# Block attention and a gated feed-forward layer on one core: the first attention units, the weight conversion and the first group in one written-out order

## The chip, the cores and the metric

The kernel runs on one core of one Trainium2 chip. Its time is the device time of one execution in microseconds. The core has five engines with a queue each, served in order: TensorE (PE in the profile, its weight loads PEld), VectorE (DVE), ScalarE (ACT), GpSimd (POOL) and SyncE (SP), which here issues all DMAs.

## What is computed

Attention over 4 batches of 8 heads, 768 tokens, head size 64. Each query sees the keys within 16 positions and, beside them, one summary key (the maximum) and one summary value (the mean) for each of 24 blocks of 32 tokens. The result, 3072 tokens by 512, goes through two matrix products with an activation between them.

```
scores_l = where(mask_l, scale * q @ k.T, -1e9)
scores_s = scale * q @ k_sum.T + log(32)        # k_sum: maximum of 32 keys
a = softmax(concat(scores_l, scores_s))
x = a @ concat(v, v_sum)                        # v_sum: mean of 32 values
h = x @ w_in                                    # 512 x 2048
g = h * tanh(log1p(exp(h)))
out = g @ w_out                                 # 2048 x 512
```

The weights come as 64-bit floats. The kernel turns each into two 32-bit parts, a high one and a low one, and does the same with x and g, so every product of the feed-forward layer is three matmuls: high by high, high by low, low by high.

## The kernel before

**Attention.** A chunk is 256 tokens of one batch (three to a batch), a unit is a chunk and a pair of heads: 12 x 4 = 48 units. A unit's work runs through the engines: scores on TensorE (`att_scores`, tile sc); mask, scale and maximum in four VectorE reductions (L279); four exponentials on ScalarE (L284); two small VectorE ops rs and the multiply of the scores by it on GpSimd (`att_normalize`, L293 to L295); a transpose on TensorE with a ScalarE copy to tile pt (`att_transpose`); the product with the values (`att_values`, x_ps), from which ScalarE makes xh and VectorE xl. The first chunk of a batch also needs km, the maximum of its keys, and vq, the mean of its values, both VectorE reductions; for batch 0 the mean is a TensorE product vm_ps. GpSimd copies km into the loaded tile qk (L225).

**Weights.** There are 16 blocks of w_in and 16 of w_out, 512 KB each in 64 bits. `load_weight` does all of a block: the DMA; on VectorE L119 and L120 (tile w_x), on ScalarE L122 (w_f), on VectorE L123 and L125, on ScalarE the copy to the high part (L127) and on GpSimd the subtraction that gives the low part (L128).

**Feed-forward.** A step in the later groups is one weight block for 512 tokens (a group is two chunks, six groups in all): `ff_in` with 12 matmuls into ph, `ff_act` (Mish on ScalarE into a), `ff_split` (ah, then al = a - ah on VectorE), and two steps later `ff_out` with 12 matmuls into four PSUM tiles po. Group 0 is done in 24 half steps of 256 tokens and two weight blocks each: the first chunk begins, the second follows four half steps behind. In group 0 ah is a ScalarE copy, later a VectorE one.

**What sets the order.** The begin and the 24 half steps of group 0 are placed by a scheduler that looks at when data is ready; the letters in the list of `begins` and the loop only give the sequence in which it is told of them. From the first step of group 1 on, the order is the program's (`manual_schedule`). Units of the next group stand at every second step of a group. Tiles come from rings (pools with a tag and a number of buffers); an instruction that writes a ring's next tile waits for the last reader of the tile that lay there.

Of the kernel before, what the change touches and what calls it, by code (L numbers as in the profile page):

```python
# [20 lines left out]
P = 128  # L21
# [15 lines left out]
NP_ = NFC // 2  # L37
LEAD = 4
# [19 lines left out]
def fused_kernel(ctx: ExitStack, tc: tile.TileContext, q0, qk, kt, v0, vw, vs, w_in, w_out, out):  # L58
# [4 lines left out]
    stage = ctx.enter_context(tc.tile_pool(name="stage", bufs=3))  # L63
# [3 lines left out]
    ff = ctx.enter_context(tc.tile_pool(name="ff", bufs=6))  # L67
# [42 lines left out]
    def load_weight(src, hi, lo, name):  # L110
        t = stage.tile([P, WP], I64, tag="stage", name=name)
        nc.sync.dma_start(t, src)
        words = t.bitcast(U32).rearrange("p (f two) -> p f two", two=2)
        low, high = words[:, :, 0], words[:, :, 1]
        f = ff.tile([P, WP], F32, tag="t", name=f"{name}_f")
        x = ff.tile([P, WP], F32, tag="t", name=f"{name}_x").bitcast(U32)
        u = f.bitcast(U32)

        nc.vector.tensor_scalar(out=x, in0=low, scalar1=29, scalar2=None, op0=ALU.logical_shift_right)  # L119
        nc.vector.scalar_tensor_tensor(out=x, in0=high, scalar=SIGN, in1=x,  # L120
                                       op0=ALU.bitwise_and, op1=ALU.bitwise_or)
        nc.scalar.activation(f, high.bitcast(F32), AF.Copy, scale=2.0 ** -OFFSET)  # L122
        nc.vector.tensor_scalar(out=f, in0=f, scalar1=-_as_f32(F32_MAX), scalar2=_as_f32(F32_MAX),  # L123
                                op0=ALU.max, op1=ALU.min)
        nc.vector.scalar_tensor_tensor(out=u, in0=u, scalar=3, in1=x,  # L125
                                       op0=ALU.logical_shift_left, op1=ALU.bitwise_or)
        nc.scalar.copy(hi, f)  # L127
        nc.gpsimd.tensor_sub(lo, f, hi.bitcast(F32))  # L128
# [36 lines left out]

    sources = {}

    def load_summaries(b, hp):

        ks = stage.tile([P, S], F32, tag="stage", name=f"ks{b}_{hp}")  # L170
        nc.sync.dma_start(ks, kt[b, hp])
        vsum = stage.tile([VP, BLK, BLK], F32, tag="stage", name=f"vsum{b}_{hp}")
        nc.sync.dma_start(vsum, vs[b, hp].rearrange("p (d j) -> p d j", j=BLK))
        sources[b, hp] = ks, vsum

    def key_summaries(b, hp):
# [11 lines left out]
        return ks  # L188

    def value_summaries(b, hp):  # L190
        vm = att.tile([KA, P], F32, tag="vm", name=f"vm{b}_{hp}", bufs=HP + 2)[KW:KA]
        summary[b, hp].append(vm)
        if b == 0:

            vwt = first_att.tile([KA, NQ, P], F32, tag="vw", name=f"vw{b}_{hp}")
            nc.sync.dma_start(vwt[0:KW], vw[b, hp].rearrange("p (s k) -> p s k", s=NQ))
            units[0, hp]["v"] = vwt
            t = first_att.tile([P, NR, P], F32, tag="v0", name=f"v{b}_{hp}", bufs=HP)
            nc.sync.dma_start(t, v0[hp].rearrange("p (j d) -> p j d", d=P))
            ps = att_psum(0, f"vm_ps{b}_{hp}")  # L200
            for j in range(NQ + NR):
                nc.tensor.matmul(ps[KW:KA, 0:P], *((blocks[0:KW, j, :], vwt[0:KW, j, :]) if j < NQ else  # L202
                                                   (blocks[:, j, :], t[:, j - NQ, :])),
                                 start=(j == 0), stop=(j == NQ + NR - 1))
# [4 lines left out]
        nc.vector.reduce_sum(vq, vsum, axis=AX.X)
# [87 lines left out]
    def att_transpose(c, hp):  # L297
# [4 lines left out]
        pt = att.tile([KA, NQ, P], F32, tag="pt", name=f"pt{c}_{hp}")  # L302
# [24 lines left out]
    def parts(step):  # L327

        if len(step) == 2:
            return [step[1]], step[0], 0, TG  # L330
        _, c, fp = step
        return [2 * fp, 2 * fp + 1], 0, c * CH, CH

    def ff_in(step):
        fcs, g, at0, n = parts(step)
        xh, xl = (x[:, :, at0:at0 + n] for x in xs[g])
        ph = ps_w.tile([P, len(fcs), n], F32, tag="w", name=f"ph{step[0]}_{step[-1]}_{at0}")
        for j, fc in enumerate(fcs):
            wh, wl = (weight(0, part, fc) for part in range(2))
            for cc in range(NCC):  # L340
                for k, (w, x) in enumerate(((wh, xh), (wh, xl), (wl, xh))):
                    nc.tensor.matmul(ph[:, j, :], w[:, cc * P:(cc + 1) * P], x[:, cc, :],  # L342
                                     start=(cc == 0 and k == 0), stop=(cc == NCC - 1 and k == 2))
        st[step] = ph.rearrange("p j t -> p (j t)")

    def ff_act(step):

        name = f"{step[0]}_{step[1]}_{step[-1]}"
        a = ff.tile([P, TG], F32, tag="t", name=f"a{name}")
        nc.scalar.activation(a, st[step], AF.Mish)  # L350
        st[step] = a, *(ff.tile([P, TG], F32R, tag=f"a{part}", name=f"a{part}{name}", bufs=3) for part in "hl")

    def ff_split(step):

        a, ah, al = st[step]

        (nc.scalar.copy if len(step) == 3 else nc.vector.tensor_copy)(ah, a)  # L357
        nc.vector.tensor_sub(al, a, ah.bitcast(F32))  # L358

    def ff_out(step):  # L360
        _, ah, al = st.pop(step)
        fcs, g, at0, n = parts(step)
        for t in range(n // P):
            row = g * TG + at0 + t * P
            if fcs[0] == 0:
                po[row] = ps_o.tile([P, DM], F32, tag="o", name=f"po{row}")
            for j, fc in enumerate(fcs):
                tok = slice(j * n + t * P, j * n + (t + 1) * P)
                wh, wl = (weight(1, part, fc) for part in range(2))
                for k, (a, w) in enumerate(((ah, wh), (al, wh), (ah, wl))):  # L370
                    nc.tensor.matmul(po[row], a[:, tok], w,  # L371
                                     start=(fc == 0 and k == 0), stop=(fc == NFC - 1 and k == 2))
            if fcs[-1] == NFC - 1:
                o = ff.tile([P, DM], F32, tag="t", name=f"o{row}")
                (nc.vector.tensor_copy if t % 2 else nc.scalar.copy)(o, po.pop(row))
                nc.sync.dma_start(out[row:row + P, :], o)
# [4 lines left out]
    steps = [(0, c, i - c * LEAD) for i in range(NP_ + LEAD) for c in range(CG) if 0 <= i - c * LEAD < NP_]
    first_steps = len(steps)
    steps += [(g, fc) for g in range(1, NG) for fc in range(NFC)]
# [3 lines left out]
    begins = {"K": lambda n: att_load_keys(0, n), "V": lambda n: att_load_values(0, n),  # L387
              "S": lambda n: (att_scores(0, n), att_normalize(0, n)), "T": lambda n: att_transpose(0, n),
              "A": lambda n: att_values(0, n), "W": load_weights, "L": lambda n: att_load(1, n)}
    for what in "K0 K1 S0 W1 K2 V0 S1 W1 T0 K3 V1 S2 A0 T1 W1 V2 S3 A1 T2 V3 A2 T3 W1 L0 A3".split():  # L390
# [109 lines left out]
```

## Time and profile before

| | |
|---|---|
| three runs | 693.78 us (692.79 to 695.2) |
| profiled execution | 693.84 us, of which the span of its instructions 692.1 us |
| busy, share of the span | TensorE 94%, VectorE 44%, ScalarE 50%, GpSimd 16% |
| chain that ended last | TensorE 81%, VectorE 9%, ScalarE 3%, DMA 3% |

A share is a mean over stages. The page cuts the span into 40 slices of 17.3 us; until about the ninth, TensorE has gaps and the other engines are busiest, and from there on TensorE is busy in nearly every tenth. The trace can be asked for the busy time of each engine in any stretch, for the chain of waits, and for the single instructions in order of time. A busy time of TensorE contains the pipelining of its matmuls, so starts are compared with starts.

### The profile page before, as it was taken

Reading aid. Unit: us, or ns where it says so; the run is one execution under the profiler, and the core shown is the slowest. Engines: PE = TensorE matmul, PEld = TensorE weight load, DVE = VectorE, ACT = ScalarE, POOL = GpSimd, SP = SyncE. Lnnn points to the kernel's source line nnn. Section 1 sums busy time; section 2 is a strip of 40 time slices with the busy share of each in tenths; the row PEclk is TensorE's granted clock in tenths of the full one; section 3 lists DMA queues with packets and bytes.
Section 4 is the critical chain, followed back from the end, with each engine's and each line's share of the span. In section 5 each row is a group of like instructions: output and inputs, shape, how many; then the busy total and the mean of one; then the engine's idle time right before and its main releaser. Section 6 shows DMA issues by size and latency. Waiting matters only on the chain.

```text
span 692.1 us, 11422 instructions
## 1 busy us (share of the span) xinstructions
PE 651.8 (94%) x4352; PEld 525.5 (76%) x4352; DVE 301.4 (44%) x884; ACT 347.7 (50%) x764; POOL 113.6 (16%) x151
## 2 busy tenths in 40 slices
PE   4876598979999999999999999999999999999997
PEld 3665476768878878878878788788788788888885
DVE  5689998883333233453232243453242232221121
ACT  3767758888754555465454464464454454111111
POOL 3444453451101001001001001001010010000000
PEclk9998789999999999999999999999999999999999
DMA  9755555764322132452122151423141110010001
GB/s 292 237 183 174 180 186 174 233 183 127 94 78 85 45 103 70 123 171 89 44 71 62 45 188 57 152 70 89 44 150 44 45 58 1 16 45 1 1 0 61
DMA packets 30678, 70.48 MB, mean 102 GB/s; under 512 B 4768, under 2 KB 9504, under 8 KB 30624
## 3 DMA queue, kind: packets, MB, share of 16 engines
q1 hardware_dynamic: 30624, 69.76, 32.1%
q8 instruction: 34, 0.56, 0.3%
q14 instruction: 20, 0.16, 0.1%
HBM read 61.15 MB, written 6.29 MB: 97 GB/s over the span
## 4 chain that ended last, share of the span: by engine, by line
PE 81%; DVE 9%; ACT 3%; DMA 3%; issue 1%; SPq 0%; POOL 0%; DVEq 0%; ACTq 0%
PE po L371 36%; PE ph L342 35%; PE x_ps L319 4%; PE sc L264 3%; PE pt_ps L301 3%; DVE w_x L119 2%; DVE w_x L120 2%; DVE w_f L123 2%; DVE w_f L125 1%; DMA w<-w_out 1%; PE vm_ps L202 1%; DMA vw<-vw 1%; ACT pr L284 1%; ACT L350 1%; DMA vsum<-vs 1%
## 5 line engine op out<-in xcount | busy, mean ns | idle before, releaser
L350 ACT ACTIVATE a<-ph 128x512 f32<-128x512 f32 x96 | 57.5, 598 | 189.3 <-PE ph L342 189.1
L295 POOL TENSOR_TENSOR pr<-pr,rs 128x480 f32<-128x480 f32 x48 | 50.4, 1050 | 391.1 <-DVE rs L294 347.5
L371 PE MATMUL po<-w_early_out_hi,ah 128*128 128x512 f32 x240 | 98.9, 418 | 12.6 <-ACT ah L357 12.4
L342 PE MATMUL ph<-xh,w_early_in_hi 128*128 128x512 f32 (+1 forms) x280 | 103.9, 371 | 1.6 <-ACT xh L320 1.6
L357 DVE CAST ah<-a 128x512 fp32r<-128x512 f32 x80 | 34.0, 425 | 159.4 <-ACT a L350 159.4
L371 PE MATMUL po<-w_early_out_hi,al 128*128 128x512 f32 x240 | 98.4, 410 | 4.9 <-DVE al L358 4.9
L342 PE MATMUL ph<-xl,w_early_in_hi 128*128 128x512 f32 (+1 forms) x280 | 101.3, 362 | 0.4 <-DVE xl L321 0.2
L342 PE MATMUL ph<-xh,w_early_in_lo 128*128 128x512 f32 (+1 forms) x280 | 101.2, 361 | 0.0
L371 PE MATMUL po<-w_early_out_lo,ah 128*128 128x512 f32 x240 | 96.8, 403 | 0.0
L321 DVE TENSOR_TENSOR xl<-x_ps,xh 128x256 fp32r<-128x256 f32 x48 | 20.2, 421 | 158.3 <-ACT xh L320 158.3
L284 ACT ACTIVATE pr<-pr,nm 128x120 f32<-128x120 f32 x192 | 73.6, 384 | 2.9 <-DVE nm L279 2.3
L358 DVE TENSOR_TENSOR al<-a,ah 128x512 fp32r<-128x512 f32 x96 | 66.5, 692 | 12.6 <-ACT ah L357 9.6
L350 ACT ACT_TABLE_LOAD x44 | 56.5, 1283 | 28.5 <-issue 14.8
L371 PEld LDWEIGHTS po<-w_early_out_hi,ah 128*128 128x128 f32 x240 | 46.0, 194 | 27.0 <-ACT ah L357 14.6
L303 ACT COPY pt<-pt_ps 120x512 f32<-120x512 f32 x48 | 28.2, 587 | 70.8 <-PE pt_ps L301 70.8
L342 PE MATMUL ph<-xh,w_late_in_hi 128*128 128x512 f32 (+1 forms) x168 | 61.8, 368 | 0.0
L342 PEld LDWEIGHTS ph<-xh,w_early_in_hi 128*128 128x128 f32 x280 | 53.1, 190 | 10.7 <-ACT xh L320 2.1
L342 PE MATMUL ph<-xh,w_late_in_lo 128*128 128x512 f32 (+1 forms) x168 | 60.6, 361 | 0.0
L342 PE MATMUL ph<-xl,w_late_in_hi 128*128 128x512 f32 (+1 forms) x168 | 60.4, 359 | 0.0
L342 PEld LDWEIGHTS ph<-xl,w_early_in_hi 128*128 128x128 f32 x280 | 53.2, 190 | 9.2 <-DVE xl L321 1.2
L371 PEld LDWEIGHTS po<-w_early_out_hi,al 128*128 128x128 f32 x240 | 47.1, 196 | 16.4 <-DVE al L358 7.4
L342 PEld LDWEIGHTS ph<-xh,w_early_in_lo 128*128 128x128 f32 x280 | 52.8, 189 | 8.9 <-issue 0.2
(76 smaller groups left out, 1055.0 us busy)
## 6 DMA issues: line engine op xcount, KB each, us to landing
qk<-qk SPq DMA_DIRECT2D x44, 496.0 KB
vw<-vw SPq DMA_DIRECT2D x48, 192.0 KB
w<-w_in SPq DMA_DIRECT2D x16, 512.0 KB
w<-w_out SPq DMA_DIRECT2D x16, 512.0 KB
ks<-kt SPq DMA_DIRECT2D x16, 384.0 KB
out<-o SPq DMA_DIRECT2D x24, 256.0 KB
vsum<-vs SPq DMA_DIRECT2D x12, 384.0 KB
vw<-vm SPq DMA_DIRECT2D x44, 48.0 KB
```

The lines of the kernel that those rows point to most:

```text
L264: nc.tensor.matmul(ps[h][row, at0:at0 + KA], u["qk"][r, s, h * QT:(h + 1) * QT], u["qk"][r, s, P:], start=True, stop=True)
L284: nc.scalar.activation(pr[:, s, :], pr[:, s, :], AF.Exp, scale=-1.0, bias=nm[:, s:s + 1], accum_out=sm[:, s:s + 1])
L295: nc.gpsimd.tensor_mul(pr, pr, rs.unsqueeze(2).broadcast_to([P, NQ, KA]))
L301: nc.tensor.transpose(ps[:KA, s * P:(s + 1) * P], u["p"][:, s, :], ident)
L303: nc.scalar.copy(pt.rearrange("p s q -> p (s q)"), ps[:KA, :])
L319: nc.tensor.matmul(x, u["v"][:, s, d], pt, start=True, stop=True)
L321: nc.vector.tensor_sub(xl, ps[:, :CH], xh.bitcast(F32))
L342: nc.tensor.matmul(ph[:, j, :], w[:, cc * P:(cc + 1) * P], x[:, cc, :], start=(cc == 0 and k == 0), stop=(cc == NCC - 1 and k == 2))
L350: nc.scalar.activation(a, st[step], AF.Mish)
L357: (nc.scalar.copy if len(step) == 3 else nc.vector.tensor_copy)(ah, a)
L358: nc.vector.tensor_sub(al, a, ah.bitcast(F32))
L371: nc.tensor.matmul(po[row], a[:, tok], w, start=(fc == 0 and k == 0), stop=(fc == NFC - 1 and k == 2))
```

## The change

All instructions now stand in the program's order. First come eight units (chunks 0 and 1), not four, with one block of weights worked on in each of ten rounds; then group 0 in 16 steps of 512 tokens like the other groups, two blocks of weights a step until there are none, with group 1's units in steps 1, 2, 3, 5, 7, 9, 11 and 13. `load_weight` is taken apart into the load, `begin_weight` (ScalarE's w_f, VectorE's w_x), `finish_weight` (VectorE's two ops on w_f, ScalarE's copy to the high part) and `lower_weight`, the subtraction for the low part, now on VectorE. A call of `load_weights(1)` lowers the block finished last, begins the next and finishes the one begun before. Key and value sources share one buffer; other rings are smaller too.

```diff
-    stage = ctx.enter_context(tc.tile_pool(name="stage", bufs=3))
+    stage = ctx.enter_context(tc.tile_pool(name="stage", bufs=2))
...
-    ff = ctx.enter_context(tc.tile_pool(name="ff", bufs=6))
+    ff = ctx.enter_context(tc.tile_pool(name="ff", bufs=4))
...
+    weights = [(0, 0)] + [(w, fc + 1 - w) for fc in range(NFC) for w in range(2) if fc + 1 - w < NFC]
...
+    def begin_weight(w, fc, t):
...
+        f = ff.tile([P, WP], F32, tag="f", name=f"w{w}_{fc}_f", bufs=3)
+        x = ff.tile([P, WP], F32, tag="t", name=f"w{w}_{fc}_x").bitcast(U32)
+        nc.scalar.activation(f, high.bitcast(F32), AF.Copy, scale=2.0 ** -OFFSET)
         nc.vector.tensor_scalar(out=x, in0=low, scalar1=29, scalar2=None, op0=ALU.logical_shift_right)
         nc.vector.scalar_tensor_tensor(out=x, in0=high, scalar=SIGN, in1=x,
                                        op0=ALU.bitwise_and, op1=ALU.bitwise_or)
-        nc.scalar.activation(f, high.bitcast(F32), AF.Copy, scale=2.0 ** -OFFSET)
+        begun.append((w, fc, f, x))
+
+    def finish_weight(w, fc, f, x):
...
         nc.vector.tensor_scalar(out=f, in0=f, scalar1=-_as_f32(F32_MAX), scalar2=_as_f32(F32_MAX),
                                 op0=ALU.max, op1=ALU.min)
         nc.vector.scalar_tensor_tensor(out=u, in0=u, scalar=3, in1=x,
                                        op0=ALU.logical_shift_left, op1=ALU.bitwise_or)
-        nc.scalar.copy(hi, f)
-        nc.gpsimd.tensor_sub(lo, f, hi.bitcast(F32))
+        nc.scalar.copy(weight(w, 0, fc), f)
+        split.append((w, fc, f))
+
+    def lower_weight(w, fc, f):
+        nc.vector.tensor_sub(weight(w, 1, fc), f, weight(w, 0, fc).bitcast(F32))
 
     def load_weights(n):
...
+        for _ in range(n):
+            if split:
+                lower_weight(*split.pop(0))
+            last = not loaded
+            if loaded:
+                begin_weight(*loaded.pop(0))
+                load_weight()
+            if len(begun) > 1 or last and begun:
+                finish_weight(*begun.pop(0))
...
-        pool, tag = (ps_o, "o") if c == 0 else (ps_w, "w")
+        pool, tag = (ps_o, "o") if c < CG else (ps_w, "w")
...
-        pt = att.tile([KA, NQ, P], F32, tag="pt", name=f"pt{c}_{hp}")
+        pt = att.tile([KA, NQ, P], F32, tag="pt", name=f"pt{c}_{hp}", bufs=1)
...
+    ctx.enter_context(tc.manual_schedule())
...
+    for u in range(n + 2):
+        if u + 1 < HP:
+            key_summary(0, u + 1, units[todo[u + 1]]["k"][:, WIN:])
+        if u < n:
+            att_scores(*todo[u])
+        if u < HP:
+            first_value_summary(u)
+        if 2 <= u:
+            att_values(*todo[u - 2])
...
+        load_weights(1)
+        if u < n:
+            att_normalize(*todo[u])
+        if HP - 2 <= u < n:
+            att_load_keys(*todo[u + 2])
+        if HP <= u:
+            att_load_values(*todo[u])
+        if 1 <= u <= n:
+            att_transpose(*todo[u - 1])
...
+    for i in range(len(steps) + 2):
+        if i < len(steps):
+            ff_in(*steps[i])
+            ff_act(*steps[i])
+        if i - 2 in at:
+            att_values(*at[i - 2])
+        if i in at:
+            att_scores(*at[i])
+        load_weights(2)
+        if i < len(steps):
+            ff_split(*steps[i])
+        if i in at:
+            att_normalize(*at[i])
+            if todo.index(at[i]) + 2 < len(todo):
+                att_load_keys(*todo[todo.index(at[i]) + 2])
...
+        if i >= 2:
+            ff_out(*steps[i - 2])
+        if i - 1 in at:
+            att_transpose(*at[i - 1])
```

Three places show what that does to the engines' queues. The first is VectorE's queue in group 0 while weights are converted; before, around a half step's al (a row names the line, the operation and the tiles, with a number for the buffer or the head pair; w_6 and w_7 are weights):

```order
L123 TENSOR_SCALAR w_7_f<-w_7_f 128x512
L321 TENSOR_TENSOR xl_309<-x_ps_1_775,xh_308 128x256
L358 TENSOR_TENSOR al_0_2_761<-a_0_2_758,ah_0_2_760 128x512
L125 SCALAR_TENSOR_TENSOR w_6_f<-w_6_f,w_6_x 128x512
L125 SCALAR_TENSOR_TENSOR w_7_f<-w_7_f,w_7_x 128x512
L293 TENSOR_SCALAR rs_3_807<-sm_3_802 128x4
L119 TENSOR_SCALAR w_7_x<-w_7_850 128x512
L123 TENSOR_SCALAR w_6_f<-w_6_f 128x512
L294 RECIPROCAL rs_3_807<-rs_3_807 128x4
L120 SCALAR_TENSOR_TENSOR w_7_x<-w_7_850,w_7_x 128x512
```

And the same queue in step 1 of group 0 now, from behind the unit's reductions to al:

```order
L143 TENSOR_TENSOR w_early_out_lo<-w_4_f,w_early_out_hi 128x512
L127 TENSOR_SCALAR w_5_x<-w_5_768 128x512
L128 SCALAR_TENSOR_TENSOR w_5_x<-w_5_768,w_5_x 128x512
L135 TENSOR_SCALAR w_6_f<-w_6_f 128x512
L137 SCALAR_TENSOR_TENSOR w_6_f<-w_6_f,w_6_x 128x512
L143 TENSOR_TENSOR w_early_in_lo<-w_6_f,w_early_in_hi 128x512
L127 TENSOR_SCALAR w_7_x<-w_7_779 128x512
L128 SCALAR_TENSOR_TENSOR w_7_x<-w_7_779,w_7_x 128x512
L135 TENSOR_SCALAR w_5_f<-w_5_f 128x512
L137 SCALAR_TENSOR_TENSOR w_5_f<-w_5_f,w_5_x 128x512
L365 TENSOR_TENSOR al_1_847<-a_1_801,ah_1_846 128x512
```

The subtraction L143 is new on this queue. The second one reads w_early_in_hi of the weight w_6 that L137, the row ahead of it, has just finished, and between the two lies ScalarE's copy.

The second place is ScalarE's queue there. Before, in the same stretch of half steps:

```order
L284 ACT_TABLE_LOAD
L284 ACTIVATE pr_3_796,sm_3_802<-pr_3_796,nm_3_797 128x120 x4
L122 ACTIVATE w_6_f<-w_6_839 128x512
L127 CAST w_early_in_hi<-w_6_f 128x512
L127 CAST w_early_in_hi<-w_7_f 128x512
L122 ACTIVATE w_7_f<-w_7_850 128x512
L127 CAST w_early_out_hi<-w_6_f 128x512
L320 CAST xh_308<-x_ps_2_913 128x256
L127 CAST w_early_out_hi<-w_7_f 128x512
```

Now, step 1:

```order
L355 ACTIVATE a_1_801<-ph_1_788 128x512
L299 ACT_TABLE_LOAD
L299 ACTIVATE pr_0_813,sm_0_819<-pr_0_813,nm_0_814 128x120 x4
L126 ACTIVATE w_5_f<-w_5_768 128x512
L139 CAST w_early_in_hi<-w_6_f 128x512
L126 ACTIVATE w_7_f<-w_7_779 128x512
L139 CAST w_early_out_hi<-w_5_f 128x512
L364 CAST ah_1_846<-a_1_801 128x512
```

The copy ah (L364) now stands behind both weights' copies L139, each of which needs VectorE's L137 of that weight.

The third place is ScalarE's queue in the first attention units. Before, the fifth and sixth unit:

```order
L284 ACTIVATE pr_0_517,sm_0_523<-pr_0_517,nm_0_518 128x120 x4
L320 CAST xh_308<-x_ps_2_422 128x256
L303 COPY pt_3_438<-pt_ps_3_433 120x512
L284 ACTIVATE pr_1_548,sm_1_554<-pr_1_548,nm_1_549 128x120 x4
L320 CAST xh_308<-x_ps_3_457 128x256
```

Now the same two:

```order
L299 ACTIVATE pr_0_450,sm_0_456<-pr_0_450,nm_0_451 128x120 x4
L335 CAST xh_325<-x_ps_2_461 128x256
L126 ACTIVATE w_1_f<-w_1_344 128x512
L139 CAST w_early_in_hi<-w_2_f 128x512
L318 COPY pt_3_498<-pt_ps_3_493 120x512
L299 ACTIVATE pr_1_510,sm_1_516<-pr_1_510,nm_1_511 128x120 x4
L335 CAST xh_325<-x_ps_3_521 128x256
```

A weight's two ScalarE ops now stand between xh and pt of every unit.

More of the change, by code (lines that the diff above doesn't have):

```diff
@@ L36 @@
 VP = NB * P // BLK
-NP_ = NFC // 2
-LEAD = 4
 CG = 2
@@ L325, in fused_kernel @@
     po = {}
[L327 to L376, printed above, removed]
@@ L379, in fused_kernel @@
-    todo = [(c, hp) for c in range(NCH) for hp in range(HP)]
[L381 to L389, printed above, removed]
@@ L436, in fused_kernel, with ff_in @@
-    with tc.manual_schedule():
-        for i in range(first_steps, len(steps) + 2):
-            if i < len(steps):
-                ff_in(steps[i])
-                ff_act(steps[i])
-            for unit in at.get(i - 2, ()):
-                att_values(*unit)
-            for unit in at.get(i, ()):
-                att_scores(*unit)
-            if i < len(steps):
-                ff_split(steps[i])
-            for unit in at.get(i, ()):
-                att_normalize(*unit)
-                load_next(keys, att_load_keys)
-                load_ahead(*unit)
-            for _ in at.get(i - 2, ()):
-                load_next(values, att_load_values)
-            ff_out(steps[i - 2])
-            for unit in at.get(i - 1, ()):
-                att_transpose(*unit)
+    def ff_in(g, fc):
+        xh, xl = xs[g]
+        ph = ps_w.tile([P, TG], F32, tag="w", name=f"ph{g}_{fc}")
+        wh, wl = (weight(0, part, fc) for part in range(2))
+        for cc in range(NCC):
+            for n, (w, x) in enumerate(((wh, xh), (wh, xl), (wl, xh))):
+                nc.tensor.matmul(ph, w[:, cc * P:(cc + 1) * P], x[:, cc, :],
+                                 start=(cc == 0 and n == 0), stop=(cc == NCC - 1 and n == 2))
+        st[g, fc] = ph
@@ new lines, in ff_out @@
+    def ff_out(g, fc):
+        ah, al = st.pop((g, fc))
+        if fc == 0:
+            po[g] = [ps_o.tile([P, DM], F32, tag="o", name=f"po{g}_{t}") for t in range(TG // P)]
+        wh, wl = (weight(1, part, fc) for part in range(2))
+        for t in range(TG // P):
+            tok = slice(t * P, (t + 1) * P)
+            for n, (a, w) in enumerate(((ah, wh), (al, wh), (ah, wl))):
+                nc.tensor.matmul(po[g][t], a[:, tok], w,
+                                 start=(fc == 0 and n == 0), stop=(fc == NFC - 1 and n == 2))
+            if fc == NFC - 1:
+                o = ff.tile([P, DM], F32, tag="t", name=f"o{g}_{t}")
+                (nc.vector.tensor_copy if t % 2 else nc.scalar.copy)(o, po[g][t])
+                nc.sync.dma_start(out[g * TG + t * P:g * TG + (t + 1) * P, :], o)
@@ new lines, in fused_kernel @@
+    todo = [(c, hp) for c in range(NCH) for hp in range(HP)]
+    steps = [(g, fc) for g in range(NG) for fc in range(NFC)]
+    at = {}
+    for u, unit in enumerate(todo[CG * HP:]):
+        g, u = divmod(u, CG * HP)
+        at[g * NFC + 2 * u - 1 if g else max(u + 1, 2 * u - 1)] = unit
+    ctx.enter_context(tc.manual_schedule())
+    first_keys(0)
+    first_keys(1)
+    load_weight()
+    first_values(0)
+    load_weight()
+    for hp in range(2, HP):
+        first_keys(hp)
+        first_values(hp - 1)
```

166 lines of the change are left out of this document (71 added, 95 removed).

## The prediction

> **What bounds the kernel now.** I read the page first (span, engine shares), then the windows by stage, then the chain of waits.
>
> ```profile
> span 692.1 us, 11422 instructions
> 50.00:75.00 25.00, 17.80 (x116) 13.72 (x115) 23.01 (x51) 19.04 (x43) 10.40 (x9) 0.77 0.63 206
> 75.00:100.00 25.00, 19.05 (x124) 15.62 (x123) 24.93 (x35) 13.31 (x23) 14.18 (x10) 0.82 0.53 169
> 183.00:286.00 103.00, 103.00 (x698) 82.49 (x693) 34.48 (x134) 54.52 (x123) 9.35 (x15) 1.00 0.28 84
> ```
>
> The columns are PE, PEld, DVE, ACT and POOL busy, the granted clock, DMA share and GB/s. Between 50 and 100 us VectorE works 23 to 24.9 of every 25 us and TensorE waits; from 183 us TensorE works without a gap and VectorE a third of the time. So there are two stages, and only the first can change much.
>
> ```profile
> 183.87 2.95 PE ph L342 x12
> 202.85 2.76 PE ph L342 x12
> 205.60 0.62 PE x_ps L319 x16
> 206.22 0.57 PE sc L264 x16
> 206.79 2.95 PE po L371 x12
> 215.21 0.43 PE pt_ps L301 x4
> 215.65 2.77 PE ph L342 x12
> ```
>
> In the chain, group 1 begins at 183.87 with its first 512-column product. From there on two steps with one attention unit take 215.65 - 202.85 = 12.8 us, all TensorE. The change keeps the matmuls, their order and the unit positions from group 1's first step, and VectorE has room there. The smaller rings (pt 1, t 4, sum 1) come round slower than a step, so I cost that part at zero. **The question is thus one number: when group 1 begins, now 183.87.** The profiled execution took 693.84 us, 1.7 around its span; the median is 693.78, so nothing hangs on which is used.
>
> **Durations.** VectorE and ScalarE rows, from stretches where GpSimd was quiet, except the two that show it busy:
>
> ```profile
> 85.85 0.68 DVE L125 SCALAR_TENSOR_TENSOR w_f<-w_f,w_x 128x512 uint32<-128x512 uint32 x1
> 86.46 0.68 DVE L358 TENSOR_TENSOR al<-a,ah 128x512 fp32r<-128x512 f32 x1
> 87.06 0.68 DVE L120 SCALAR_TENSOR_TENSOR w_x<-w,w_x 128x512 uint32<-128x512 uint32 x1
> 92.31 0.41 DVE L123 TENSOR_SCALAR w_f<-w_f 128x512 f32<-128x512 f32 x1
> 92.76 0.69 DVE L125 SCALAR_TENSOR_TENSOR w_f<-w_f,w_x 128x512 uint32<-128x512 uint32 x1
> 141.22 0.41 DVE L119 TENSOR_SCALAR w_x<-w 128x512 uint32<-128x512 uint32 x1
> 141.56 0.41 DVE L321 TENSOR_TENSOR xl<-x_ps,xh 128x256 fp32r<-128x256 f32 x1
> 87.26 2.22 POOL L128 TENSOR_TENSOR w_early_in_lo<-w_f,w_early_in_hi 128x512 fp32r<-128x512 f32 x1 [3.49 <-ACT w_early_in_hi L127]
> 88.26 1.50 DVE L119 TENSOR_SCALAR w_x<-w 128x512 uint32<-128x512 uint32 x1
> 86.56 0.62 ACT L127 CAST w_early_in_hi<-w_f 128x512 fp32r<-128x512 f32 x1 [0.24 <-DVE w_f L125]
> 87.09 0.69 ACT L122 ACTIVATE w_f<-w 128x512 f32<-128x512 f32 x1
> ```
>
> Starts lie closer than lengths: a two-input VectorE op blocks the next for 0.60 (86.46 to 87.06), a one-input op for 0.45 when the next needs its result (92.31 to 92.76), xl for about 0.34. ScalarE's copies follow each other after 0.53 (86.56 to 87.09), and a copy starts 0.03 after the VectorE op it needs (85.85 + 0.68 = 86.53).
>
> **What goes.** GpSimd's 32 lower-part subtractions (L128) leave, and with them the stretch they put on VectorE: L119 takes 1.50 beside one, 0.41 alone. The new subtraction has al's shape, so I take al's 0.68, 0.60 to the next start. The means show what that stretch is worth:
>
> ```profile
> L119 DVE TENSOR_SCALAR w_x<-w 128x512 uint32<-128x512 uint32 x32 | 25.3, 812 | 3.6 <-DMA w<-w_in 2.3 <-DMA w<-w_out 1.2
> L120 DVE SCALAR_TENSOR_TENSOR w_x<-w,w_x 128x512 uint32<-128x512 uint32 x32 | 28.6, 908 | 0.1
> L125 DVE SCALAR_TENSOR_TENSOR w_f<-w_f,w_x 128x512 uint32<-128x512 uint32 x32 | 25.9, 819 | 0.2
> L123 DVE TENSOR_SCALAR w_f<-w_f 128x512 f32<-128x512 f32 x32 | 19.5, 616 | 1.1 <-ACT w_f L122 1.1
> ```
>
> Together 99.3 us. After: 0.60 + 0.45 + 0.60 + 0.45 + 0.68 = **2.78 per weight**, 89 us for 32 with the subtraction included. VectorE's work falls by 10 us although it gets more of it.
>
> **What comes: waits.** In the new order VectorE's subtraction stands right behind the op that finishes the same weight, whose ScalarE copy (L139) it needs. VectorE is served in order, so it stands still for 0.03 + 0.62 + 0.05 = 0.70. In a group 0 step there are two weights, then ScalarE's copy ah, then al. From the first subtraction to the end of ah: 2.78 + 0.70 + 2.78 + (0.03 + 0.53 + 0.62) = **7.44**. With al behind it (0.65 with its wait) a step costs 8.1 us before any attention, against 2.76 + 2.95 on TensorE.
>
> The attention unit's ops in a step:
>
> ```profile
> 132.92 0.28 DVE L279 CUSTOM_DVE_ANT_0 pr<-sc,base 128x120 f32<-128x120 f32 x1
> 133.73 0.69 DVE L120 SCALAR_TENSOR_TENSOR w_x<-w,w_x 128x512 uint32<-128x512 uint32 x1
> L294 DVE RECIPROCAL rs<-rs 128x4 f32<-128x4 f32 x48 | 8.5, 176 | 1.4
> 144.36 0.94 DVE L186 TENSOR_REDUCE km<-ks 128x24 f32<-128x768 f32 x1
> 136.94 1.21 DVE L209 TENSOR_REDUCE vq<-vsum 96x32 f32<-96x1024 f32 x1
> 139.66 0.43 DVE L210 TENSOR_SCALAR vq<-vq 96x32 f32<-96x32 f32 x1
> 133.24 0.40 ACT L284 ACTIVATE pr<-pr,nm 128x120 f32<-128x120 f32 x1 [1.04 <-DVE nm L279]
> 134.88 1.28 ACT L350 ACT_TABLE_LOAD   x1
> 136.17 0.60 ACT L350 ACTIVATE a<-ph 128x512 f32<-128x512 f32 x1
> 138.22 0.37 ACT L320 CAST xh<-x_ps 128x256 fp32r<-128x256 f32 x1
> 143.79 0.59 ACT L303 COPY pt<-pt_ps 120x512 f32<-120x512 f32 x1 [1.07 <-PE pt_ps L301]
> 147.24 0.99 POOL L295 TENSOR_TENSOR pr<-pr,rs 128x480 f32<-128x480 f32 x1 [0.78 <-DVE rs L294]
> ```
>
> VectorE: four score reductions 0.85 (132.92 to 133.73, and a start), two rs ops 0.40, km 0.95, the vq pair 1.55, xl 0.36. ScalarE: four exponentials 1.6 (133.24 to 134.88), table load 1.29, Mish 0.5 to the next start.
>
> **Group 0, counted from its first ff_in.** The first ah ends at 11.8: the last unit's xh and xl end at 0.8, VectorE's weight behind them at 3.6, its hi at 4.2; VectorE then runs 2.78 + 0.70 + 2.78 + 1.18, and ScalarE's table load and Mish (until 6.1) lie beside that but for some 0.1. Step 1: al 0.65, scores 0.9, 7.44 = 9.0. Step 2 adds rs 0.4, and ScalarE, with Mish, exponentials and two table loads, is 0.6 late for hi: 10.0. In steps 3 and 4 xl waits for xh, which stands behind pt 0.6, a table load 1.29, Mish 0.5 and its own 0.37, so that xl ends 3.2 after the last ah; with scores 0.9 (step 3 only) and 7.44 that is 11.6 and 10.6. Odd steps from 5: al, vq, xl, scores, 7.44 = 10.9 (three times). Even steps from 6: al, rs, km, 7.44 = 9.4 (three times). Step 11 has one weight left: 6.4. Sum 11.8 + 41.2 + 32.7 + 28.2 + 6.4 = 120.3. GpSimd keeps the multiply (L295) and the km copy; I add 0.6 a unit for VectorE ops beside them, 3.6: **124**. TensorE cannot run ahead: ff_out waits for al two steps back, the transpose for rs one step back. After the last ah come al 0.65, rs 0.40, the multiply 0.99 and the transpose 0.43, with waits 2.6, and steps 13 to 15 at TensorE's pace (3 x 5.7 plus units, 20.0): 146.6 from ff_in to group 1.
>
> **Eight units first.** The unit's ring through two in-order engines: exponentials 1.6, xh 0.37, 0.05, xl 0.34, one weight 2.78, 0.03, hi 0.53, pt 0.59 = **6.3 per unit**, and 0.3 more for units that also copy a small vm. Nothing overlaps: ScalarE reaches the next exponentials only behind pt, pt stands behind hi, hi needs VectorE's weight, and that stands behind xl, which needs this unit's xh. VectorE is busy 4.4 of the 6.3. For the start:
>
> ```profile
> 10.91 1.87 PE L202 MATMUL vm_ps<-vw,blocks 96*24 96x128 f32 x8 [4.32 <-DMA vw<-vw]
> 13.94 1.90 PE L202 MATMUL vm_ps<-v,blocks 128*24 128x128 f32 x8
> ```
>
> Before, vm's loads landed at 10.9; the new order puts 512 KB fewer ahead of them, so about 10, and the products take 3.8; behind them stand the second unit's scores (1.9), its VectorE ops and weight, and the first pt copy: about 20. Then 2 x 6.6 and 4 x 6.3 give 58.4; the seventh unit without exponentials 5.4; the last x product 0.6. First ff_in at **64**, between 57 (loads and start quicker) and 72 (TensorE slow). Loads do not bind: a weight, qk and vw are 512, 496 and 192 KB by their shapes, 1.25 MB a unit in 6.3 us or 200 GB/s, and the first window above moved 206. A weight is loaded a whole unit, later a whole step, before it is used.
>
> **Sum:** group 1 at 64 + 146.6 = 210.6 instead of 183.87, so 693.84 + 26.7 = **720 us**, 3.8% slower.
>
> **A price only a page states.** The table load above takes 1.29 from start to start of its neighbours. The Trainium skill ("ScalarE: Activation LUTs", What ACT_TABLE_LOAD costs) gives about 2.66 us with a drain. By that price steps 1 to 4 would grow by some 8 us and the sum be 728, an estimate; the row decides, and the trace disagrees with the page here.
>
> **Rivals.** *VectorE's work alone decides (faster).* If the waits vanish, a unit costs 0.85 + 0.4 + 0.34 + 2.78 = 4.4 and a step 2 x 2.78 + 0.65 = 6.2 plus attention. The first ff_in falls by 8 x 1.9 to about 49. Group 0 takes 11 x 6.2, 6 units at 1.6, four km and vq at 2.5, 3.6 beside GpSimd, some 5 for start and step 11, and the 22.6 at the end, about 119: group 1 at 168, total **678**. For it: 89 us of weights instead of 99, and TensorE would be ready. Against it: the order puts consumer right behind producer's copy. It decides from the point where fewer than 16 of the 42 us of waits remain.
>
> *TensorE at half clock (slower still).* The windows show clock 0.77 and 0.82 where TensorE was busy 18 to 19 of 25 us. In the new first stretch it has 1.6 us of work in 6.3, and 13 us in 20 after. Were every step at half speed, two steps would take 25.6 instead of 20.3, 30 us more over eleven steps: **750**. The Trainium skill ("TensorE: Matmul & The Clock Gate", HAM oscillation) says that idle gaps over about 3.4 us bring the half clock back. By that rule the first stretch runs at half clock, and group 0 only in part, since at half clock it is busy.
>
> *The stretch stays.* If L119 to L125 keep their means for another reason than GpSimd, 0.9 us a weight (99.3 / 32 less 2.2) comes on top: about 750. The 0.41 and 1.50 speak against it.
>
> **Chances.** Forecast with its own range 705 to 740: 0.62 (first ff_in 57 to 72, a step 0.7 either way). Waits half absorbed, 690 to 705: 0.12, in it 0.05 within 0.3% of before (what a measurement can tell) and 0.02 below. Rival at 678: 0.16. The two slow ones, 740 to 755: 0.10. Faster 0.18, same 0.05, slower 0.77. The range 690 to 745 leaves out the rival at 678 and the end of the slow cases.
>
> **What would show it.** First ff_in near 64, group 1 near 211; steps 5 to 10 alternating 10.9 and 9.4 us; VectorE idle before the subtraction (L143) and al (L365), released by ScalarE's copies, about 0.7 and 1.2 each; L127 and L128 near 0.43 and 0.68; two steps in 12.8 from group 1. Wrong if L143 hardly waits, if first ff_in is before 55, or if later groups lose time to the smaller rings.

## The result, and the profile after

The changed kernel takes 723.94 us (median of four runs, 723.14 to 728.07) beside 694.49 of the kernel before: 1.042 times its time, with a 95% interval of 1.035 to 1.049. The profiled execution took 723.14 us, 1.84 around its span.

First the page of the changed kernel: its span, and each engine's busy time.

```profile
span 721.3 us, 10972 instructions
PE 652.5 (90%) x4160; PEld 520.2 (72%) x4160; DVE 297.3 (41%) x916; ACT 337.5 (47%) x754; POOL 64.4 (9%) x119
PE 73%; DVE 14%; ACT 7%; DMA 4%; issue 2%; SPq 0%; ACTq 0%; DVEq 0%
```

The third line is the chain that ended last, by engine. TensorE's part of it falls from 81% to 73%, VectorE's rises from 9% to 14% and ScalarE's from 3% to 7%, although VectorE's busy share is lower than before (41% for 44%). The loss is thus no added work on these engines; it is work waiting for other work.

Where it lies is read from the two starts on which the prediction rests, the first ff_in and that of group 1. The first row is from the instructions in order of time, the others from the chain of waits (start, length, what).

```profile
64.41 0.80 PE L348 MATMUL ph<-xh,w_early_in_hi 128*128 128x512 f32 x1
...
199.87 2.76 PE ph L348 x12
...
212.74 2.76 PE ph L348 x12
```

Group 0 begins at 64.41 and group 1 at 212.74, 28.9 us later than before. From there to the end of the span it is 721.3 - 212.74 = 508.6 us; before it was 692.1 - 183.87 = 508.2. So all of the loss lies ahead of group 1. The last two steps of group 0 take 212.74 - 199.87 = 12.87 us, the pace of the later groups.

The windows show the stages (PE, PEld, DVE, ACT and POOL busy, granted clock, DMA share, GB/s): the attention rounds, the weight steps of group 0, its last steps.

```profile
20.00:64.00 44.00, 21.19 (x267) 15.88 (x267) 27.46 (x94) 22.90 (x76) 8.99 (x12) 0.60 0.59 195
75.00:190.00 115.00, 82.59 (x463) 63.47 (x462) 84.61 (x205) 71.84 (x148) 9.28 (x14) 0.84 0.50 159
190.00:212.00 22.00, 22.00 (x154) 17.53 (x153) 4.80 (x23) 12.42 (x27) 1.20 (x2) 1.00 0.15 46
```

Before, VectorE worked 23 to 24.9 of every 25 us in its weight stage. Now it works 84.61 of 115, and TensorE does not fill the rest: both stand still in turn. In the last row it is the other way round: TensorE works without a gap, VectorE 4.80 of 22.

What the standing still looks like is seen in one step, on VectorE's queue (start, length, line, and in brackets the idle time before it and what ended it):

```profile
131.97 0.95 DVE L143 TENSOR_TENSOR w_early_out_lo<-w_f,w_early_out_hi 128x512 fp32r<-128x512 f32 x1
132.84 0.41 DVE L127 TENSOR_SCALAR w_x<-w 128x512 uint32<-128x512 uint32 x1
133.29 0.69 DVE L128 SCALAR_TENSOR_TENSOR w_x<-w,w_x 128x512 uint32<-128x512 uint32 x1
133.90 0.42 DVE L135 TENSOR_SCALAR w_f<-w_f 128x512 f32<-128x512 f32 x1
134.35 0.69 DVE L137 SCALAR_TENSOR_TENSOR w_f<-w_f,w_x 128x512 uint32<-128x512 uint32 x1
135.72 0.69 DVE L143 TENSOR_TENSOR w_late_in_lo<-w_f,w_late_in_hi 128x512 fp32r<-128x512 f32 x1 [0.68 <-ACT w_late_in_hi L139]
...
139.81 0.69 DVE L365 TENSOR_TENSOR al<-a,ah 128x512 fp32r<-128x512 f32 x1 [1.20 <-ACT ah L364]
```

Starts lie as close as foreseen (0.45, 0.61 and 0.45 from 132.84 on), and the two waits stand where foreseen, with 0.68 and 1.20. The first subtraction waits for nothing, since its weight was finished a step earlier; the second reads the weight finished just ahead of it.

### The profile page after: what moved, and what is told of

Same layout as the page of the kernel before. It is cut to its first block, busy times and chain, and to the rows that moved or that the text cites. A ratio compares the mean times of both kernels' runs of the same rounds, so it can differ in the third digit from the quotient of the medians.

```text
span 721.3 us, 10972 instructions
## 1 busy us (share of the span) xinstructions
PE 652.5 (90%) x4160; PEld 520.2 (72%) x4160; DVE 297.3 (41%) x916; ACT 337.5 (47%) x754; POOL 64.4 (9%) x119
## 4 chain that ended last, share of the span: by engine, by line
PE 73%; DVE 14%; ACT 7%; DMA 4%; issue 2%; SPq 0%; ACTq 0%; DVEq 0%
PE po L376 34%; PE ph L348 31%; PE x_ps L334 4%; DVE w_f L137 3%; PE sc L279 3%; DVE w_x L128 3%; PE pt_ps L316 2%; DVE w_f L135 1%; ACT pr L299 1%; DVE w_x L127 1%; DMA vw<-vw 1%; ACT pt L318 1%; DVE w_early_in_lo L143 1%; DMA vw<-vm 1%; ACT ah L364 1%
## 5 line engine op out<-in xcount | busy, mean ns | idle before, releaser
L364 DVE CAST ah<-a 128x512 fp32r<-128x512 f32 x80 | 34.0, 425 | 172.1 <-ACT a L355 172.1
L348 PE MATMUL ph<-xh,w_early_in_hi 128*128 128x512 f32 x240 | 99.4, 414 | 0.0
L348 PE MATMUL ph<-xh,w_early_in_lo 128*128 128x512 f32 x240 | 96.3, 401 | 0.0
L348 PE MATMUL ph<-xl,w_early_in_hi 128*128 128x512 f32 x240 | 96.2, 401 | 0.0
L334 PE MATMUL x_ps<-pt,vw 120*64 120x64 f32 x768 | 36.4, 244 | 34.7 <-ACT pt L318 34.1
L334 PEld LDWEIGHTS x_ps<-pt,vw 120*64 120x64 f32 x768 | 29.4, 151 | 52.5 <-ACT pt L318 39.9
L376 PE MATMUL po<-w_late_out_hi,ah 128*128 128x512 f32 x144 | 58.0, 403 | 0.0
L348 PE MATMUL ph<-xh,w_late_in_hi 128*128 128x512 f32 x144 | 57.7, 401 | 0.0
L348 PE MATMUL ph<-xh,w_late_in_lo 128*128 128x512 f32 x144 | 56.6, 393 | 0.0
L348 PE MATMUL ph<-xl,w_late_in_hi 128*128 128x512 f32 x144 | 56.4, 392 | 0.0
L376 PE MATMUL po<-w_late_out_hi,al 128*128 128x512 f32 x144 | 56.4, 392 | 0.0
```

What stands on the lines that cost most here:

```text
L334: nc.tensor.matmul(x, u["v"][:, s, d], pt, start=True, stop=True)
L348: nc.tensor.matmul(ph, w[:, cc * P:(cc + 1) * P], x[:, cc, :], start=(cc == 0 and n == 0), stop=(cc == NCC - 1 and n == 2))
L364: (nc.scalar.copy if g == 0 else nc.vector.tensor_copy)(ah, a)
L376: nc.tensor.matmul(po[g][t], a[:, tok], w, start=(fc == 0 and n == 0), stop=(fc == NFC - 1 and n == 2))
```

## The experiments

One number carries the argument, the length of group 0 from its first ff_in to group 1's first, so it stands beside each time. Group 1's start is the ff_in in the chain of waits that lies 507.7 to 509.6 us ahead of the span's end; those rows are over 5 us apart. Each ratio is to the kernel before, run beside it on the same chip (its medians 693.9 to 695.3).

| kernel | median us | ratio (95%) | first ff_in | group 1 | group 0 |
|---|---|---|---|---|---|
| changed | 723.94 | 1.042 (1.035 to 1.049) | 64.41 | 212.74 | 148.3 |
| ah_first | 715.47 | 1.029 (1.023 to 1.034) | 65.05 | 204.17 | 139.1 |
| lower_later | 714.60 | 1.028 (1.022 to 1.033) | 63.13 | 202.95 | 139.8 |
| both_moved | 703.76 | 1.012 (1.007 to 1.016) | 64.98 | 193.74 | 128.8 |
| weight_before_values | 716.64 | 1.028 (1.024 to 1.033) | 57.18 | 206.27 | 149.1 |
| all_three | 696.53 | 1.000 (0.997 to 1.003) | 57.94 | 186.18 | 128.2 |
| after_spread | 711.57 | 1.024 (1.018 to 1.029) | 63.60 | 200.33 | 136.7 |
| spread_weights | 683.90 | 0.984 (0.980 to 0.989) | 55.81 | 172.50 | 116.7 |
| lower_on_gpsimd | 726.69 | 1.045 (1.040 to 1.050) | 64.68 | 215.56 | 150.9 |
| before_lower_on_vector | 686.76 | 0.985 (0.981 to 0.989) | | 177.31 | |

The first three kernels take out the two waits of a weight step without taking out work.

**The copy ah moved ahead of the weights (ah_first).** ScalarE makes ah as soon as it can, so that al finds it ready.

```diff
         if i in at:
             att_scores(*at[i])
+        if i < NFC:
+            ff_high(*steps[i])
         load_weights(2)
         if i < len(steps):
             ff_split(*steps[i])
```

> ScalarE's copy ah of group 0 stands ahead of the step's two weights instead of behind them; nothing else moves. Waits theory (VectorE stands still behind ScalarE's copies): al no longer waits 1.2 us in eleven steps, so group 1 begins 11 to 13 us earlier, about 201, and the time is 711 to 714 us. Rival (VectorE's work alone sets the step): nothing changes, 722 to 727. Rival (TensorE at half clock sets it): at most 3 us.

Measured: 8.5 us shorter, all of it in group 0 (9.2). In the weight steps the wait at al is gone, yet the gain is smaller than expected, and 715.47 lies outside the 711 to 714 given. Two steps of this kernel on VectorE (al is now L370, and stands where a new step's work begins behind it):

```profile
84.32 0.68 DVE L370 TENSOR_TENSOR al<-a,ah 128x512 fp32r<-128x512 f32 x1
91.51 0.69 DVE L143 TENSOR_TENSOR w_early_in_lo<-w_f,w_early_in_hi 128x512 fp32r<-128x512 f32 x1 [2.38 <-ACT w_early_in_hi L139]
94.25 0.68 DVE L370 TENSOR_TENSOR al<-a,ah 128x512 fp32r<-128x512 f32 x1
...
163.19 0.69 DVE L370 TENSOR_TENSOR al<-a,ah 128x512 fp32r<-128x512 f32 x1
171.49 0.69 DVE L370 TENSOR_TENSOR al<-a,ah 128x512 fp32r<-128x512 f32 x1
```

The late step takes 171.49 - 163.19 = 8.3 us where its counterpart took 9.6: the whole wait is gained. The early one takes 9.93, as long as it did before (9.94). There ScalarE is the one behind, and its own queue shows why:

```profile
85.07 1.28 ACT L355 ACT_TABLE_LOAD   x1
...
86.98 1.28 ACT L299 ACT_TABLE_LOAD   x1
...
89.81 0.60 ACT L361 CAST ah<-a 128x512 fp32r<-128x512 f32 x1
...
90.88 0.60 ACT L139 CAST w_early_in_hi<-w_f 128x512 fp32r<-128x512 f32 x1
```

Behind two table loads, Mish and the exponentials, ah now stands ahead of the weight's copy and delays it; VectorE waits 2.38 at L143 for what it no longer waits at al. In step 2 the wait was handed on, not removed. Steps 1, 3 and 4 got only 0.4 to 0.5 shorter; in steps 3 and 4 VectorE's xl waits 0.8 longer for ScalarE's xh, which now stands behind ah (2.45 and 1.61 for 1.67 and 0.83). The size I gave was too large by those steps.

**The subtraction moved to the next call (lower_later).** A weight is lowered one call after it was finished, so its ScalarE copy has a whole weight's time.

```diff
-            if split:
+            if len(split) > 1 or split and not loaded and not begun:
                 lower_weight(*split.pop(0))
```

> The subtraction for the low part is taken one call later, so its high part is long copied. Waits theory: the wait of 0.7 us once a step goes, eleven times, 7 to 8 us: 715 to 718 us, first ff_in unchanged at 64. Work theory: no change, 722 to 727.

Measured: 9.3 us shorter, 8.5 of it in group 0. No wait of L143 for L139 is left in the waits between 20 and 190 us; before they came to 9.3 us in 13 waits (below). A little more than expected was gained.

The waits of the changed kernel between 20 and 190 us (who for whom, us in total, times, longest):

```profile
DVE al L365 <- ACT ah L364: 13.2, 11, 1.2
DVE w_late_in_lo L143 <- ACT w_late_in_hi L139: 4.1, 6, 0.7
DVE w_early_in_lo L143 <- ACT w_early_in_hi L139: 3.8, 5, 1.1
DVE w_late_out_lo L143 <- ACT w_late_out_hi L139: 0.7, 1, 0.7
DVE w_early_out_lo L143 <- ACT w_early_out_hi L139: 0.7, 1, 0.7
```

**Both edits (both_moved).**

> Both moves at once. Waits theory: a step falls from 8.1 to 6.2 us before attention, together about 20 us: 702 to 706 us, a little less gained if ScalarE's two table loads in steps 1 to 4 become the limit. Work theory: 722 to 727.

Measured: 20.2 us shorter, group 0 by 19.6. The two waits together are 13.2 + 9.3 = 22.5 us in the rows above, of which 20 come back. Alone the edits gave 9.2 and 8.5 in group 0, 17.7; together they give 2 more. Of VectorE's waits at L143, one of which ah had lengthened in ah_first, none is left.

**The order of a round (weight_before_values).** In the first ten rounds the weight and the normalization come ahead of the previous unit's value products, so that VectorE's weight ops no longer stand behind xl, which waits for this round's xh.

```diff
+        load_weights(1)
+        if u < n:
+            att_normalize(*todo[u])
         if 2 <= u:
             att_values(*todo[u - 2])
...
-        load_weights(1)
-        if u < n:
-            att_normalize(*todo[u])
```

> In the first ten rounds the weight's calls stand ahead of the unit's value product, so VectorE works on the weight while ScalarE does the exponentials. Ring theory (exponentials, xh, xl, weight, hi, pt one behind the other): a round falls from 6.15 to about 5.0 us, first ff_in near 56 instead of 64.4, the time 714 to 718 us. If loads or TensorE at half clock set the round: first ff_in stays at 63 to 65, 722 to 727.

Measured: 7.3 us shorter; the first ff_in comes 7.2 us earlier and group 0 keeps its length (149.1 for 148.3). In the changed kernel a round's ring is seen in the chain (here one round without its weight's five VectorE operations, then the start of the next and of the last):

```profile
26.25 1.52 ACT pr L299 x8
28.48 0.42 DVE xl L336
...
32.25 0.58 ACT pt L318
32.83 1.52 ACT pr L299 x8
...
51.24 1.52 ACT pr L299 x8
```

Four rounds from 26.25 to 51.24 are 6.25 us each on average. ScalarE, VectorE, ScalarE stand one behind the other in every one. In weight_before_values the exponentials begin at 25.14, 30.95, 37.16, 42.08 and 47.00, 5.5 each on average and 4.9 in the last two. The first two are longer because TensorE is on the chain there, with the products for vm (3.38 us from 24.99) and with scores (1.21 us from 35.64).

**All three (all_three).**

> The new order with all three moves: ah first, subtraction later, weight ahead of the values. Waits theory: the gains add up, 13 + 8 + 8 us: 693 to 698 us, about the time of before. Work theory: 714 to 727.

Measured: 27.4 us shorter than the changed kernel, the sum of 20.2 and 7.3, and equal to the kernel before (0.997 to 1.003). So three moves that only change the order of the instructions are worth 27 of the 29 us that the change lost. They explain the loss against the kernel before. They do not yet give a gain, although the move of the subtraction to VectorE is worth 7 us in the old order (before_lower_on_vector below): against that kernel some 10 us are still lost, and spreading the weights (spread_weights below) wins about as much.

**Fewer weights in a step (after_spread, spread_weights).** The last steps of group 0 leave VectorE idle. Odd steps now take one weight instead of two, once in the changed kernel as it is, once with the three moves.

```diff
-        load_weights(2)
+        load_weights(2 if i % 2 == 0 else 1)
```

> The changed kernel with nothing moved, but one weight in odd steps instead of two. Theory (each weight with its waits lengthens the step that it stands in, and the last five steps of group 0 have VectorE nearly idle): about five weights move from steps 1 to 10 into steps 11 to 14, each taking 2.78 us of work and 0.7 of waiting out of a step set by VectorE: up to 17 us shorter; 706 to 714. Rival (the round trips by ScalarE set a step's length whatever the number of weights): 718 to 726.

> All three reorderings, and in the 512-token steps two weights in even steps but one in odd steps, so that the weights reach to step 14 instead of step 10. In the run with all three reorderings VectorE was busy 74.8 of 85 us between 75 and 160 and TensorE 68.9, while from 160 to 186 TensorE was busy without a gap and VectorE only 5.3 of 26. Theory (in group 0 the sum of VectorE's work in the weight steps sets the time, and VectorE's idle last steps are free room): TensorE's work in group 0 is 14.95 + 68.9 + 26.0 = 110 of 129 us, so at most 17 us can go; 8 to 14 us shorter, 682 to 689. Rival (the later weights come so close to the step that reads them that TensorE waits for them at steps 13 to 15): 692 to 698, with TensorE waiting for w_late tiles near 160 to 185.

Measured: group 0 gets 11.6 us shorter in the one (148.3 to 136.7) and 11.5 in the other (128.2 to 116.7). TensorE does not wait for late weights: in its last steps it has no gap. The rows of the stage between 75 and 160 us and of the end, first of all_three, then of spread_weights:

```profile
75.00:160.00 85.00, 68.93 (x415) 53.77 (x416) 74.75 (x175) 63.77 (x130) 7.95 (x12) 0.88 0.65 201
160.00:186.00 26.00, 26.00 (x171) 20.80 (x170) 5.34 (x24) 13.55 (x32) 2.65 (x4) 1.00 0.16 47
```

```profile
75.00:160.00 85.00, 75.62 (x487) 60.01 (x488) 69.83 (x173) 64.36 (x132) 8.70 (x13) 0.92 0.64 204
160.00:173.00 13.00, 13.00 (x86) 10.41 (x85) 8.99 (x24) 10.50 (x22) 1.66 (x2) 1.00 0.20 60
```

VectorE's busy share falls from 88% to 82% between 75 and 160 us and rises from 21% to 69% in the rest of group 0, where it now has weights too; TensorE's rises from 81% to 89% in the first of the two. What VectorE's queue looks like when nothing stands in its way is seen in a step of spread_weights with two weights:

```profile
106.17 0.68 DVE L143 TENSOR_TENSOR w_early_out_lo<-w_f,w_early_out_hi 128x512 fp32r<-128x512 f32 x1
...
108.90 0.68 DVE L143 TENSOR_TENSOR w_early_in_lo<-w_f,w_early_in_hi 128x512 fp32r<-128x512 f32 x1
...
111.63 0.68 DVE L370 TENSOR_TENSOR al<-a,ah 128x512 fp32r<-128x512 f32 x1
```

Two weights now take 111.63 - 106.17 = 5.46 us instead of the 7.84 from 131.97 to 139.81 above: 2.73 each, with no idle time. At 683.90 us this version is faster than the kernel before and the changed one: 0.984 of the former's time (0.980 to 0.989).

**Which engine subtracts (lower_on_gpsimd, before_lower_on_vector).** The change did two things at once: a written-out order, and the subtraction on VectorE. One kernel is the changed one with the subtraction back on GpSimd, the other the kernel before, with its scheduler's order, with the subtraction on VectorE.

```diff
-        nc.vector.tensor_sub(weight(w, 1, fc), f, weight(w, 0, fc).bitcast(F32))
+        nc.gpsimd.tensor_sub(weight(w, 1, fc), f, weight(w, 0, fc).bitcast(F32))
```

```diff
-        nc.gpsimd.tensor_sub(lo, f, hi.bitcast(F32))
+        nc.vector.tensor_sub(lo, f, hi.bitcast(F32))
```

> The new order with the subtraction on GpSimd as before. Stretch theory (GpSimd's subtraction slows VectorE's ops beside it): the four VectorE ops of a weight go back from 2.2 to about 3.1 us, 29 us more, against 19 us of subtractions and 8 us of waits gone: 720 to 735 us, mean of L127 near 0.8. If the stretch before came from something else: L127 stays at 0.42 and the time is 695 to 705.

> The kernel before with nothing changed but the engine of the subtraction; the scheduler may place it anew. If VectorE's work bounds the first 150 us there, about 10 us of it go (stretch of GpSimd against 32 subtractions): 680 to 688 us. If the subtraction brings its waits along whatever the order: 694 to 705.

In the kernel before, the move makes it 1.5% faster (0.981 to 0.989); group 1 begins at 177.31 instead of 183.87. The scheduler also placed other instructions of VectorE and ScalarE anew, so the number holds for both together. Its groups show what left (line, operation, count, busy us, mean ns):

```profile
L120 DVE SCALAR_TENSOR_TENSOR w_x<-w,w_x 128x512 uint32<-128x512 uint32 x32 | 26.1, 830 | 0.0
L125 DVE SCALAR_TENSOR_TENSOR w_f<-w_f,w_x 128x512 uint32<-128x512 uint32 x32 | 21.8, 697 | 0.0
L123 DVE TENSOR_SCALAR w_f<-w_f 128x512 f32<-128x512 f32 x32 | 13.9, 435 | 1.6 <-ACT w_f L122 1.4
L119 DVE TENSOR_SCALAR w_x<-w 128x512 uint32<-128x512 uint32 x32 | 13.7, 453 | 5.1 <-DMA w<-w_out 3.2 <-DMA w<-w_in 1.9
```

The four are 75.5 us instead of 99.3. So this part of the change is good in the old order, and the new order lost what it gained and 29 us more. It also puts the best version into its place: spread_weights, at 0.984 of the kernel before, can't be told from this one-line edit at 0.985, since the intervals overlap.

In the changed order GpSimd costs only 2.8 us more than VectorE, which the intervals of the two ratios don't separate. The total came as expected, but not by the way that I had expected, a stretch of L127 to 0.8 us. The groups between 20 and 190 us:

```profile
L135 DVE TENSOR_SCALAR w_f<-w_f 128x512 f32<-128x512 f32 x31 | 23.9, 772 | 0.0
L127 DVE TENSOR_SCALAR w_x<-w 128x512 uint32<-128x512 uint32 x30 | 14.9, 497 | 3.2 <-DMA w<-w_out 3.2
L365 DVE TENSOR_TENSOR al<-a,ah 128x512 fp32r<-128x512 f32 x12 | 12.2, 1018 | 27.4 <-ACT ah L364 27.4
```

L127 has 0.50, and most of the stretch falls on L135, which stands beside the subtraction here (0.77; 0.43 with the subtraction on VectorE). The waits at al double, from 13.2 to 27.4 us. One of them is 5.39 us long, and the queues of GpSimd and ScalarE show where it comes from:

```profile
138.28 0.26 POOL L247 COPY qk<-km 128x96 f32<-128x96 f32 x1 [6.35 <-DMA qk<-qk]
138.50 1.26 POOL L143 TENSOR_TENSOR w_early_out_lo<-w_f,w_early_out_hi 128x512 fp32r<-128x512 f32 x1
...
139.80 0.66 ACT L126 ACTIVATE w_f<-w 128x512 f32<-128x512 f32 x1 [5.14 <-POOL w_early_out_lo L143]
...
141.04 1.26 POOL L143 TENSOR_TENSOR w_late_out_lo<-w_f,w_late_out_hi 128x512 fp32r<-128x512 f32 x1
```

GpSimd's small copy into the loaded tile waits 6.35 us for its DMA, and three subtractions stand behind it. ScalarE's L126 writes the next tile of the ring w_f and waits 5.14 us for the first of them, which still reads the tile that lies there; ah and with it al stand behind L126. In a fixed order each engine's queue passes on the waits of whatever stands at its head. The run therefore mixes two things, the stretch and this queue, and says nothing of either alone.

## Why the prediction was right

Group 1 was foreseen at 210.6 and came at 212.74; the profiled execution was foreseen at 720 and took 723.14.

- **One number decides.** Held: 508.6 us from group 1 to the end beside 508.2. The smaller rings cost nothing that can be seen, and two steps still take 12.8.
- **The first stretch.** Foreseen: 6.3 us per round and the first ff_in at 64. Measured: 6.25 on average and 64.41. That the ring through two engines sets it, not the loads, is shown by weight_before_values, which leaves the order of the loads as it is and ends the stretch at 57.18.
- **The weights.** 2.78 us each: the step above has 135.72 - 131.97 = 3.75 with 0.68 of waiting and 0.26 from a subtraction that took 0.95 beside GpSimd's multiply, which leaves 2.8.
- **The waits.** Foreseen: 0.70 and 1.2. Measured: 0.68 to 0.69 and 1.20 in most steps. both_moved shows that they cost nearly what they last: 22.5 us of them, 20 won back.
- **The steps.** The copies ah, on ScalarE, give the lengths; the row L127, of VectorE, is from step 5:

```profile
75.66 0.61 ACT L364 CAST ah<-a 128x512 fp32r<-128x512 f32 x1
...
116.42 0.61 ACT L364 CAST ah<-a 128x512 fp32r<-128x512 f32 x1
...
123.30 0.43 DVE L127 TENSOR_SCALAR w_x<-w 128x512 uint32<-128x512 uint32 x1 [2.46 <-DMA w<-w_out]
...
129.58 0.61 ACT L364 CAST ah<-a 128x512 fp32r<-128x512 f32 x1
139.16 0.61 ACT L364 CAST ah<-a 128x512 fp32r<-128x512 f32 x1
...
186.18 0.61 ACT L364 CAST ah<-a 128x512 fp32r<-128x512 f32 x1
```

The first ends 11.86 after ff_in (11.8 foreseen); steps 1 to 4 take 40.8 together (41.2), step 6 takes 9.6 (9.4). Only step 5 is off by more than 0.4, 13.2 for 10.9, because VectorE waited 2.46 us there for a weight's DMA. That a weight is loaded a whole step before its use was no proof that it has landed.

Three terms were mis-sized and partly cancel, so that group 0 came as near as 148.3 for 146.6 is in part luck. The DMA wait (2.3 us) was missing. The 3.6 us for VectorE operations beside GpSimd were too much: steps 1 to 11 take 186.18 - 75.66 = 110.5 us, of which 2.3 are the DMA wait, and 108.5 was foreseen without the 3.6. What the rows show of that stretch is some 0.26 at the subtraction in four of the steps (0.94 or 0.95 for 0.69) and under 0.1 elsewhere, and slightly shorter terms make up for it. The end was too short: behind the last weight's ah come four steps at TensorE's pace (12 to 15), not three; from the end of that copy, 186.79, to 212.74 it is 26.0 us where 22.6 was foreseen. Sum: +2.3 - 3.6 + 3.4 = 2.1 us, where group 0 was 1.7 longer; the rest are small differences.

- **The rival of VectorE's work alone.** It did not come about, because the order put each consumer right behind the producer's copy. Its price was also too low: with the three moves and the weights where the change has them (all_three), the first ff_in comes at 57.94 where the rival gave 49, group 0 takes 128.2 where it gave 119, and the kernel takes 696.5 us where it gave 678. Only with the weights spread as well, which the rival did not foresee, does it come to 684.
- **The half clock.** The clock did fall as that rival said: 0.60 in the first stretch in the windows above. It cost little there, since TensorE was not what the round waited for (below). In the weight steps the clock was 0.84 and the time of the steps was VectorE's and ScalarE's; in step 9, where two products of TensorE lie on the chain at half clock (1.12 and 1.08 us), the step is 0.65 us longer than step 7. It fell between 28 and 29 us, when TensorE had stood still for at most 1.4 us (since 27.57), and stayed at 0.50 through waits of 0.8 to 2.1 us in the rounds from 32.9 to 51.3. The rule of the Trainium skill that was weighed ("TensorE: Matmul & The Clock Gate", HAM oscillation), that idle gaps over about 3.4 us bring the half clock back, agrees with the trace in direction only: here shorter gaps went with it.
- **The stretch stays.** It did not: between 20 and 190 us L127 has a mean of 0.42 and L128 of 0.69.

## What to carry to other kernels

When an order is written out by hand, look in each engine's queue for a consumer that stands right behind another engine's short copy of what was just made: each such pair costs the copies between them and the handovers, here 0.7 us with one copy and 1.2 with two, and an engine that is busy three quarters of the time can then be the bound. Moving the consumer one item later, or the copy ahead of unrelated work, takes no instruction away and gave 20 us here; but a copy moved up also goes ahead of something, so the gain ends where its engine is the later one. And work that only has to be done by some step is spread over the steps that have room, not done as early as possible: here that gave 11.6 us, as much with the waits as without them.

## What the runs showed of the hardware

- **Half clock and a round.** In the changed kernel the granted clock was 0.50 from 29 to 69 us. The 16 products with the values took 0.69 us at the clock of 1.00 (from 26.30) and 1.12 at 0.50 (from 39.04). What that does to a round is best seen in weight_before_values, where two rounds of the same kind, from 37.16 and from 42.08, had clocks of 0.82 and 0.53 and took 4.92 us each. A slower TensorE is hidden in a round on whose chain it does not lie.
- **Some VectorE operations wait for GpSimd's whole operation.** In lower_on_gpsimd, between 20 and 190 us, the 128x512 one-input operation L135 took 0.41 to 0.48 us in 21 cases and 1.48 to 1.52 in the other ten, each of which ran beside one of GpSimd's subtractions; the mean of 0.77 hides that. The al that follows the three subtractions shown above begins under the last of them (141.04 to 142.30):

```profile
141.52 1.34 DVE L365 TENSOR_TENSOR al<-a,ah 128x512 fp32r<-128x512 f32 x1 [5.39 <-ACT ah L364]
```

It ends at 142.86, 0.56 after GpSimd does: nearly its own length behind the other's end, not both at half speed. The subtraction took 1.26, as the first of the three did while VectorE stood still. The Trainium skill ("SBUF — State Buffer", SBUF: two separate sides) says that the port pair that these two engines share is held for a whole instruction and that the loser blocks; this row agrees. It is not so of every operation: in the changed kernel the reduction km took 0.92 (131.13 to 132.05) beside a GpSimd multiply of 0.98 (from 131.38). In the kernel before it took 0.94 with GpSimd idle at its start (144.36), and the multiplies of the changed kernel between 20 and 215 us are all 0.98 or 0.99. So where two such operations meet, the stretch goes to the one that runs at that moment, and moving an operation moves the stretch to another line.
- **The start differs from run to run by about 2 us.** all_three and spread_weights have the same program up to the first ff_in, which came at 57.94 and 55.81. It isn't the chip alone: lower_later and both_moved, the same up to there too and run on one chip, have 63.13 and 64.98. Comparisons of a few us are better made from ff_in than from the span.
